# A linear attention, GLU and MLP kernel on one core: weight sums of the GLU stages moved behind a DMA, and one hidden slice's products staged and copied by ScalarE alone

## The chip, the core and the metric

One core of a Trainium2 chip runs the whole program. The metric is device time in microseconds (us). TensorE multiplies matrices, VectorE and ScalarE do elementwise work, GpSimd does elementwise work and issues some of the DMAs (transfers between on-chip memory and DRAM), SyncE (SP) issues the others. Each engine takes its instructions strictly in the order in which the program holds them.

## The reference

```python
x  = linear_attention(q, k, v, omega)     # 4 x 8 heads x 576 tokens x 64 -> 2304 x 512
xn = x / sqrt(mean(x*x, -1) + 1e-6) * rms_g
g  = xn @ w_gate                          # 2304 x 1536
y  = (g * sigmoid(g) * (xn @ w_val)) @ w_out      # 2304 x 512
h  = y @ w2_in                            # 2304 x 2048
out = (h * sigmoid(h)) @ w2_out           # 2304 x 512
```

The weight matrices come as float64, the other arrays as float32.

## The kernel before, in words

**Blocks and slices.** The 2304 tokens are five blocks: 0 to 3 of 512 tokens, and block 4, the short block, of 256. Blocks 0 to 2 are called early (`NE` = 3). The hidden dimension of the GLU is 12 slices f of 128, that of the MLP 16. Each product runs as three TensorE passes (high x high, high x low, low x high), for which each operand is split into a high and a low fp32r half: ScalarE copies the high half (`split_h` L198 for hidden values, `split_hi` L463 for weights, `tok_high` L385 for token sums), and VectorE subtracts it for the low half (L199, L467, L388).

**A weight slice** is loaded by SP as raw words (`raw`), decoded to `m` by five VectorE operations (L146 to L157) and two integer adds on GpSimd (L160), scaled by rms_g on ScalarE (L168, four operations), and split.

**Phases.** Attention and the first two GLU slices run in an order written out by hand until about 180 us. Then the *passage* (`stream`) takes the rest of these slices for blocks 3 and 4 and the third slice, f2, for the blocks in the order 1, 0, 2, 3, 4. For each block there are 12 matmuls each for gate and value (`g1_glu`, `proj`), silu on ScalarE (L222), a multiply on VectorE (L228), the split, and the output product in four quarters of 128 output columns (`g2_glu`, quarters d = 0 to 3, L267). Quarters of blocks 0 and 2 go into a stage tile (`w_2`, `w_3`): even quarters by ScalarE (L278), odd ones by VectorE (L280). After each pair a GpSimd DMA (L281) adds the tile to the block's rows of `out` in DRAM, which serve as an accumulator (`kept`). Those of block 1 are instead added by VectorE to the on-chip tile `ya` (L287), which GpSimd DMAs then write out (L776). The passage also makes four *token sums* of blocks 0 and 1 (L393 adds the halves, L396 and L388 subtract).

**GLU stages.** Slices 3 to 11 are units u = 0 to 8. The four full blocks are done by `quad`, a scheme of seven products for eight that needs the token sums and two *weight sums* (`sum12`, `sum34`: four operations `less` of 128x256 on GpSimd, L362). `WeightQueue.plan` lists the weight jobs of each unit; one job (a tuple) is issued at each tick, between TensorE's pieces. The output products of the unit before (`pend`) are interleaved, and the short block has plain projections (L205) in the middle, with L696 (multiply for the first half) just ahead of the next output product.

**Standard units.** u = 9 is the first MLP unit (`std`); the transition to it is at 555 to 600 us. There `g2_glu` with `last` adds the final slice (L287), and splits the result into `xs` (high by ScalarE, L291, low by `low`, L257: GpSimd for block 1, VectorE otherwise).

`wait` holds the short block's split; `flush` issues it.

Of the kernel before, what the change touches and what calls it, by code (L numbers as in the profile page):

```python
# [20 lines left out]
def kernel(  # L21
# [14 lines left out]
    nc = tc.nc  # L36
# [176 lines left out]
    def proj(w, j, ps):  # L213
        yield 3 * KC * blocks[j] / 2365
        part(w, j, ps, 0, 3 * KC)

    def g1_glu(f, j, hs, mid):
        wq.need((1, "g", f))
        p = ps_tile("ps_g" if blocks[j] == TB * P else "ps_y", [P, blocks[j]])
        yield from proj(wt[1, "g", f], j, p)  # L220
        s = pools["s"][0].tile([P, blocks[j]], F32, tag="s", name="s", bufs=pools["s"][1])
        nc.scalar.activation(out=s, in_=p, func=AF.Silu)  # L222
        if blocks[j] == TB * P:
            yield from mid
        wq.need((1, "v", f))
        p = ps_tile("ps_g" if blocks[j] == TB * P else "ps_y", [P, blocks[j]])
        yield from proj(wt[1, "v", f], j, p)
        nc.vector.tensor_tensor(out=s, in0=s, in1=p, op=ALU.mult)  # L228
        if mid is None:
            wait.append(lambda: hs.update({f: split_h(s, j)}))  # L230
            return
        hs[f] = split_h(s, j)
        if blocks[j] < TB * P:
            yield from mid
# [11 lines left out]
    def kept(j, n):  # L246
        r0 = j * TB * P + 2 * n * P
        return out[r0:r0 + 2 * P, :].rearrange("(p r) d -> p (r d)", r=2)

    def g2_glu(fs, j, hs, first, last, keep=None):  # L250
        wq.need(*[(1, "o", f) for f in fs])
        staged = j < NE and not last and keep is None
        y = ya[j].rearrange("p (c t) -> p c t", c=KC)
        nn = 3 * len(fs)

        def low(d):
            (nc.gpsimd if j == 1 else nc.vector).tensor_tensor(  # L257
                out=xs[j][:, 1, d, :], in0=y[:, d, :],
                in1=xs[j][:, 0, d, :].bitcast(F32), op=ALU.subtract,
            )  # L260

        for d in range(KC):
            ps = ps_tile("ps_y", [P, blocks[j]])
            n = 0
            for f in fs:
                for a, c in PASS:
                    nc.tensor.matmul(  # L267
                        out=ps,
                        lhsT=wt[1, "o", f][:, a, d * P:(d + 1) * P],
                        rhs=hs[f][:, c, :],  # L270
                        start=(n == 0),
                        stop=(n == nn - 1),
                    )
                    n += 1
            if staged:
                if d % 2 == 0:
                    o = stage()
                    nc.scalar.activation(out=o[:, 0, :], in_=ps, func=AF.Copy)  # L278
                else:
                    nc.vector.tensor_copy(out=o[:, 1, :], in_=ps)  # L280
                    nc.gpsimd.dma_start(  # L281
                        out=kept(j, d // 2), in_=o.rearrange("p t d -> p (t d)"), accum_op=ALU.add
                    )
            elif first:
                nc.scalar.activation(out=y[:, d, :], in_=ps, func=AF.Copy)
            else:
                nc.vector.tensor_tensor(out=y[:, d, :], in0=ps, in1=y[:, d, :], op=ALU.add)  # L287
            if keep and d % 2:
                keep(j, d // 2)
            if last:  # L290
                nc.scalar.activation(out=xs[j][:, 0, d, :], in_=y[:, d, :], func=AF.Copy)  # L291
                if d:
                    low(d - 1)
            yield nn * blocks[j] / 2365
        if last:
            low(KC - 1)
# [122 lines left out]
    class WeightQueue:  # L419
# [28 lines left out]
        def plan(self, u):  # L448
# [25 lines left out]
            def lo(key):  # L474
                split_lo(mf(key), st[key].t)
                wt[key] = st[key].t
# [37 lines left out]
            elif kind == 1:  # L514
# [5 lines left out]
                    (1, lambda: hi(a1)),  # L520
                    (0, lambda: lo(a1)),
                    (1, lambda: hi(a0)),
                    (0, lambda: lo(a0), sum12),
                    (0, sum34),
                    (1, lambda: shi(0)),
                    (0, lambda: slo(0), lambda: dec(bs[0], 0), lambda: load(u + 1, 0, 0)),
                    (1, lambda: shi(1)),
# [3 lines left out]
            elif std <= u < std + NSTD:  # L531
# [2 lines left out]
                jobs = [  # L534
                    *head,
                    (0, lambda: dec(a0, 0), lambda: load(u, bs[0], 0)),
                    (0,),
                    (1, lambda: hi(a1)),
                    (0, lambda: lo(a1)),
                    *[(0, lambda: dec(bs[1], 1), lambda: load(u + 1, 1, 1))] * (u > std),  # L540
                    (1, lambda: hi(a0)),
                    (0, lambda: lo(a0)),
                    *[(0, lambda: dec(bs[1], 1), lambda: load(u + 1, 1, 1))] * (u == std),
                    (0, lambda: dec(bs[0], 0), lambda: load(u + 1, 0, 0)),
# [227 lines left out]
    def stream():  # L772
        f0, (f2,) = sweeps[0][1], sweeps[1][1]

        def keep(j, n):
            (nc.gpsimd if j == 1 else nc.sync).dma_start(out=kept(j, n), in_=ya[j][:, 1024 * n:1024 * (n + 1)])  # L776

        for j in (0, 2):
            for n in range(2):
                keep(j, n)  # L780
        pend = ()
        wq.rest = 1.25
        order = [(3, f0), (4, f0), (1, [f2]), (0, [f2]), (2, [f2]), (3, [f2]), (4, [f2])]
# [19 lines left out]
        for n, (j, fs) in enumerate(order):  # L803
# [14 lines left out]
                stages[:] = [wq.slot(("y", k), F32) for k in range(2)]  # L818
            if n == 5:
                sums.extend(later23)  # L820
            out = g2_glu(fs, j, hs, j >= NE and fs is f0, False, keep if j == 1 else None)
            pend = chain_of(pend, flush(), out) if mine else out
        wq.free += [(1, 0), (1, 1)]
        for u, (kind, fs) in enumerate(groups):
            first, last = kind == 2 and fs[0] == 0, u == len(groups) - 1
# [896 lines left out]
```

## Time and profile before

| | |
|---|---|
| runs | 962.07, 962.36, 960.64 us, median 962.07 us |
| profiled execution | 960.27 us; its span 958.5 us |
| TensorE busy | 935.2 us, 98% of the span |
| VectorE | 720.0 us, 75% |
| ScalarE | 524.7 us, 55% |
| GpSimd | 461.8 us, 48% |
| DMA | 128.60 MB, mean 134 GB/s |

The span is that of the profiled execution from its first to its last instruction; the time beside it is the same execution's device time, 1.8 us more. Busy shares are means over phases with different limits. In the timelines below a line gives the start and the length in us, the engine, the source line and the operation as out<-in; several equal instructions in a row are one line (x2), whose length runs from the first one's start to the last one's end; the bracket is the engine's idle time ahead of it and what ended it.

### The profile page before, as it was taken

What the parts mean: (1) busy time and instruction counts of PE and PEld (TensorE: products, weight loads), DVE (VectorE), ACT (ScalarE), POOL (GpSimd) and SP (SyncE); (2) the same over time, 40 slices, a digit from 0 to 9 for tenths busy, and PEclk for the clock granted to TensorE, in tenths of its full rate; (3) what the DMA queues carried; (4) which work ended last, traced back from release to release, by engine and by line L of the source; (5) the groups of instructions that cost most, each with busy time, mean ns of one, the idle gap of its engine ahead of it and who ended that gap; (6) DMA issues with size and microseconds to landing.
All of it is one profiled execution on the core that took longest, in us unless ns stands there. A gap on an engine that the chain in (4) does not pass through costs nothing.

```text
span 958.5 us, 17354 instructions
## 1 busy us (share of the span) xinstructions
PE 935.2 (98%) x6480; PEld 777.8 (81%) x6480; DVE 720.0 (75%) x1335; ACT 524.7 (55%) x1149; POOL 461.8 (48%) x491
## 2 busy tenths in 40 slices
PE   8999999997999999999999998999999999999998
PEld 6888878885788888888888876888888888888887
DVE  6998999777777977877877887977775757575634
ACT  5999877544355355454454445546545444445442
POOL 8888655005335535435434423556544545454411
PEclk9999999998999999999999999999999999999999
DMA  7655443205437658648648650546868787868778
GB/s 186 170 132 148 138 128 100 95 26 152 88 66 162 133 102 175 134 88 185 129 94 184 133 199 1 158 150 131 164 128 169 130 171 129 167 131 160 118 143 172
DMA packets 98500, 128.60 MB, mean 134 GB/s; under 512 B 29424, under 2 KB 75760, under 8 KB 98416
## 3 DMA queue, kind: packets, MB, share of 16 engines
q0 software_dynamic: 17280, 59.78, 35.4%
q1 hardware_dynamic: 80864, 67.65, 25.0%
q8 instruction: 51, 0.84, 0.4%
q14 instruction: 33, 0.27, 0.1%
q10 hardware_dynamic: 272, 0.07, 0.0%
HBM read 54.59 MB, written 68.16 MB: 128 GB/s over the span
## 4 chain that ended last, share of the span: by engine, by line
PE 82%; DVE 8%; ACT 3%; POOL 2%; DMA 2%; issue 1%; SPq 1%; DVEq 0%; POOLq 0%; ACTq 0%
PE g L602 28%; PE y L319 20%; PE y L267 12%; PE g L205 4%; PE b L1190 3%; PE y L205 3%; PE b L205 2%; DVE s L696 2%; PE b L1374 2%; PE kv L1270 2%; PE b L1163 2%; PE b L1590 2%; POOL m L160 1%; ACT h L198 1%; DVE h L199 1%
## 5 line engine op out<-in xcount | busy, mean ns | idle before, releaser
L160 POOL TENSOR_TENSOR m<-m,raw 128x512 int32<-128x512 int32 x136 | 202.8, 1492 | 239.9 <-issue 114.0
L319 PE MATMUL y<-w,h 128*128 128x512 f32 (+1 forms) x870 | 212.2, 388 | 0.6 <-DVE h L199 0.3
L319 PEld LDWEIGHTS y<-w,h 128*128 128x128 f32 x870 | 161.9, 188 | 34.7 <-DVE h L199 0.9
L602 PE MATMUL g<-xs,w 128*128 128x512 f32 x720 | 181.7, 390 | 0.0
L267 PE MATMUL y<-h,w 128*128 128x512 f32 (+1 forms) x648 | 157.1, 377 | 14.7 <-ACT h L198 7.8
L199 DVE TENSOR_TENSOR h<-s,h 128x512 fp32r<-128x512 f32 (+1 forms) x125 | 89.6, 728 | 98.2 <-ACT h L198 98.1
L602 PEld LDWEIGHTS g<-xs,w 128*128 128x128 f32 x720 | 134.2, 188 | 27.3
L267 PEld LDWEIGHTS y<-h,w 128*128 128x128 f32 x648 | 116.0, 192 | 44.3 <-ACT h L198 10.7
L344 POOL DMA_DIRECT2D out_dram<-ya x64 | 58.7, 990 | 116.9 <-DVE ya L338 47.3
L198 ACT ACTIVATE h<-s 128x512 fp32r<-128x512 f32 (+1 forms) x125 | 74.0, 597 | 59.4 <-DVE s L228 27.0
L336 ACT ACTIVATE ya<-y 128x512 f32<-128x512 f32 x82 | 48.2, 593 | 69.0 <-PE y L319 60.2
L205 PE MATMUL g<-xs,w 128*128 128x512 f32 x336 | 80.9, 391 | 0.2 <-DVE xs L257 0.2
L338 DVE COPY ya<-y 128x512 f32<-128x512 f32 x52 | 35.7, 687 | 59.4 <-PE y L319 59.4
L281 POOL DMA_DIRECT2D out_dram<-w x52 | 45.3, 871 | 72.5 <-ACT w L278 68.4
L1239 ACT ACTIVATE e<-b,nb 128x128 f32<-128x128 f32 x272 | 75.8, 423 | 7.5 <-issue 4.1
L205 PEld LDWEIGHTS g<-xs,w 128*128 128x128 f32 x336 | 62.8, 189 | 13.9 <-DVE xs L257 1.0
L614 ACT ACTIVATE g<-g 128x512 f32<-128x512 f32 x60 | 34.9, 581 | 70.7 <-PE g L602 70.1
L467 DVE TENSOR_TENSOR w<-m,w 128x512 fp32r<-128x512 f32 x74 | 69.2, 935 | 3.5 <-ACT w L463 3.5
L629 ACT ACTIVATE s<-s 128x512 f32<-128x512 f32 x42 | 26.6, 632 | 80.0 <-DVE s L634 80.0
L602 PE MATMUL g<-w,w 128*128 128x512 f32 x270 | 69.9, 395 | 0.0
L602 PE MATMUL g<-ya,w 128*128 128x512 f32 x270 | 68.5, 389 | 0.0
L205 PEld LDWEIGHTS y<-xs,w 128*128 128x128 f32 x480 | 60.2, 188 | 2.0
(139 smaller groups left out, 1589.7 us busy)
## 6 DMA issues: line engine op xcount, KB each, us to landing
out_dram<-ya POOLq DMA_DIRECT2D x54, 512.0 KB, 6.8
out_dram<-w POOLq DMA_DIRECT2D x54, 512.0 KB, 7.0
raw<-in_moe_w_out_dram SPq DMA_DIRECT2D x28, 512.0 KB, 4.4
raw<-in_moe_w_in_dram SPq DMA_DIRECT2D x16, 512.0 KB, 4.4
raw<-in_moe_w_gate_dram SPq DMA_DIRECT2D x12, 512.0 KB, 4.1
raw<-in_moe_w_val_dram SPq DMA_DIRECT2D x12, 512.0 KB, 4.6
out_dram<-ya SPq DMA_DIRECT2D x12, 512.0 KB, 5.1
qT<-e SPq DMA_DIRECT2D x72, 64.0 KB, 2.3
```

The source lines that it names most:

```text
L160: tt(out=mi, in0=mi, in1=(low if step == 5 else high).bitcast(I32), op=ALU.add)
L198: nc.scalar.activation(out=ht[:, 0, :], in_=s, func=AF.Copy)
L199: nc.vector.tensor_tensor(out=ht[:, 1, :], in0=s, in1=ht[:, 0, :].bitcast(F32), op=ALU.subtract)
L205: nc.tensor.matmul(out=ps, lhsT=w[:, a, cc * P:(cc + 1) * P], rhs=xs[j][:, c, cc, :], start=(n == 0), stop=(n == 3 * KC - 1),)
L267: nc.tensor.matmul(out=ps, lhsT=wt[1, "o", f][:, a, d * P:(d + 1) * P], rhs=hs[f][:, c, :], start=(n == 0), stop=(n == nn - 1),)
L281: nc.gpsimd.dma_start(out=kept(j, d // 2), in_=o.rearrange("p t d -> p (t d)"), accum_op=ALU.add)
L319: nc.tensor.matmul(out=ps, lhsT=hs[f][:, a, t * P:(t + 1) * P], rhs=wt[2, "p", f][:, c, d0:d1], start=(n == 0), stop=(n == nn - 1),)
L336: nc.scalar.activation(out=o[:, t % 2, :], in_=ps, func=AF.Copy)
L344: nc.gpsimd.dma_start(out=rows, in_=o[p0:p1], accum_op=ALU.add)
L467: eng.tensor_tensor(out=v[:, 1, :], in0=x, in1=v[:, 0, :].bitcast(F32), op=ALU.subtract)
L602: nc.tensor.matmul(out=ps, lhsT=w[:, a, (c0 + c) * P:(c0 + c + 1) * P], rhs=x(b, c), start=(start and n == 0), stop=(n == 3 * KH - 1), ski ...
L1239: nc.scalar.activation(out=st.e[r][:, :, h, :] if blocks4 else st.e[r][:, h, :], in_=src.rearrange("p (a f) -> p a f", a=4) if blocks4 els ...
```

## The change

What the diff does, edit by edit:

1. `proj2` cuts the 12-matmul projections of `g1_glu` into two pieces of 6, so there are more ticks between which other engines' work is issued.
2. Block 1's third slice is staged like those of blocks 0 and 2; its rows are written to `out` early by SP instead of by GpSimd later, and the four VectorE adds (L287) go.
3. `calm`: the third slice's products of blocks 0 to 2 are copied by ScalarE alone.
4. In the plan of a GLU unit (u from 1) `sum12` leaves its job and is issued with `sum34` in the next one.
5. In the plan of unit 9 an empty job goes, and the low half of one weight is issued with the high half of the other.
6. `low` for block 2 goes to GpSimd too.
7. The short block's waiting split is flushed after two quarters of block 3's output product instead of four.

```diff
@@ proj2
+    def proj2(w, j, ps):
+        for n in (0, 6):
+            yield 6 * blocks[j] / 2365
+            part(w, j, ps, n, n + 6)
...
-        yield from proj(wt[1, "g", f], j, p)
+        yield from proj2(wt[1, "g", f], j, p)
...
-        yield from proj(wt[1, "v", f], j, p)
+        yield from proj2(wt[1, "v", f], j, p)
@@ g2_glu
-        staged = j < NE and not last and keep is None
+        staged = j < NE and not last
...
-            (nc.gpsimd if j == 1 else nc.vector).tensor_tensor(
+            (nc.gpsimd if 0 < j < NE else nc.vector).tensor_tensor(
...
-                    nc.scalar.activation(out=o[:, 0, :], in_=ps, func=AF.Copy)
+                if d % 2 == 0 or calm:
+                    nc.scalar.activation(out=o[:, d % 2, :], in_=ps, func=AF.Copy)
                 else:
                     nc.vector.tensor_copy(out=o[:, 1, :], in_=ps)
+                if d % 2:
...
-            if keep and d % 2:
-                keep(j, d // 2)
@@ plan, GLU units
-                    (0, lambda: lo(a0), sum12),
-                    (0, sum34),
+                    (0, lambda: lo(a0)),
+                    (0, sum12, sum34),
@@ plan, standard units
-                    (0,),
+                    *[(0,)] * (u > std),
                     (1, lambda: hi(a1)),
-                    (0, lambda: lo(a1)),
+                    *[(0, lambda: lo(a1))] * (u > std),
...
-                    (1, lambda: hi(a0)),
+                    (1, *[lambda: lo(a1)] * (u == std), lambda: hi(a0)),
@@ stream
-        for j in (0, 2):
+        for j in (0, 2, 1):
             for n in range(2):
-                keep(j, n)
+                nc.sync.dma_start(out=kept(j, n), in_=ya[j][:, 1024 * n:1024 * (n + 1)])
...
-            out = g2_glu(fs, j, hs, j >= NE and fs is f0, False, keep if j == 1 else None)
-            pend = chain_of(pend, flush(), out) if mine else out
+            out = g2_glu(fs, j, hs, j >= NE and fs is f0, False, fs is f0 or j < NE)
+            pend = chain_of(take(pend, 2), flush(), pend, out) if mine else out
```

TensorE's order does not change. The other engines' orders change at three kinds of place. In the rows below, line numbers of the changed kernel are 5 to 8 higher than those of the same statement before.

VectorE in the passage, between the first five decode operations and the multiply and split ahead of block 0's output product. `m` and `raw` are the weight being decoded, `ya_95` is block 1's output tile, `ya_96` and `w_1` are token-sum tiles. Before:

```order
L287 TENSOR_TENSOR ya_95<-y,ya_95 128x512 x2
L396 TENSOR_TENSOR ya_96<-ya_96 128x1024
L287 TENSOR_TENSOR ya_95<-y,ya_95 128x512
L396 TENSOR_TENSOR ya_96<-ya_96,w_1_3921 128x1024
L228 TENSOR_TENSOR s<-s,g 128x512
L199 TENSOR_TENSOR h<-s,h 128x512
L146 TENSOR_SCALAR m_4025<-raw_3974 128x512
```

and in the changed kernel:

```order
L398 TENSOR_TENSOR ya_96<-xs_92 128x1024
L401 TENSOR_TENSOR ya_96<-ya_96 128x1024
L146 TENSOR_SCALAR m_4013<-raw_3962 128x512
L149 TENSOR_SCALAR raw_3962<-raw_3962 128x512
L152 TENSOR_SCALAR m_4013<-m_4013 128x512
L154 TENSOR_SCALAR raw_3962<-raw_3962 128x512
L157 TENSOR_SCALAR m_4013<-m_4013 128x512
L233 TENSOR_TENSOR s<-s,g 128x512
L199 TENSOR_TENSOR h<-s,h 128x512
L401 TENSOR_TENSOR ya_96<-ya_96,w_1_3923 128x1024
```

The four adds to `ya_95` are gone; two token sums (L398 and L401) and the second weight's decode now stand ahead of the multiply (L228, now L233).

ScalarE in the passage, about ten instructions up to the split ahead of block 2's output product. `w_2` and `w_3` are stage tiles, `ya_96` to `ya_4075` token sums. Before:

```order
L198 ACTIVATE h<-s 128x512
L385 ACTIVATE ya_4023<-ya_96 128x1024
L222 ACTIVATE s<-g 128x512
L278 ACTIVATE w_2_3950<-y 128x512
L385 ACTIVATE ya_4055<-ya_96 128x1024
L168 ACTIVATE m_3976<-m_3976,g_sb 128x128 x4
L463 ACTIVATE w_4_4061<-m_3976 128x512
L278 ACTIVATE w_3_3951<-y 128x512
L168 ACTIVATE m_4025<-m_4025,g_sb 128x128 x4
L463 ACTIVATE w_5_4089<-m_4025 128x512
L198 ACTIVATE h<-s 128x512
```

and in the changed kernel:

```order
L198 ACTIVATE h<-s 128x512
L168 ACTIVATE m_3964<-m_3964,g_sb 128x128 x4
L468 ACTIVATE w_4_4039<-m_3964 128x512
L390 ACTIVATE ya_4047<-ya_96 128x1024
L227 ACTIVATE s<-g 128x512
L284 ACTIVATE w_2_3951<-y 128x512 x2
L284 ACTIVATE w_3_3952<-y 128x512
L390 ACTIVATE ya_4075<-ya_96 128x1024
L168 ACTIVATE m_4013<-m_4013,g_sb 128x128 x4
L468 ACTIVATE w_5_4081<-m_4013 128x512
L284 ACTIVATE w_3_3952<-y 128x512
L198 ACTIVATE h<-s 128x512
```

All four copies of block 0's product are now here (L284; two before, L278), the last of them right ahead of the split (L198), and a wait for GpSimd's write of `ya` has no counterpart (the second token sum's copy now comes ahead of the second scale). Block 1's four copies stand in the two rows before this piece.

GpSimd in one GLU stage, with the semaphores that each row waits for; `ws` is the weight sum's tile, `m_4581` and `m_4613` (now `m_4583` and `m_4615`) the two weights. Before:

```order
L281 DMA out_dram<-w_0_4518 128x1024 [waits DMASW5_49,DVE_49,Activation_49]
L281 DMA out_dram<-w_2_3950 128x1024 [waits DMASW6_49,DVE_49,Activation_49]
L362 TENSOR_TENSOR ws<-m_4581 128x256
L362 TENSOR_TENSOR ws<-ws,m_4613 128x256 [waits Pool_49]
L281 DMA out_dram<-w_3_3951 128x1024 [waits DMASW7_49,DVE_49,Activation_49]
L362 TENSOR_TENSOR m_4581<-m_4613,m_4581 128x256
L362 TENSOR_TENSOR m_4581<-m_4613,ws 128x256 [waits Pool_49]
```

and in the changed kernel:

```order
L288 DMA out_dram<-w_0_4520 128x1024 [waits DMASW5_49,DVE_49,Activation_49]
L288 DMA out_dram<-w_2_3951 128x1024 [waits DMASW6_49,DVE_49,Activation_49]
L288 DMA out_dram<-w_3_3952 128x1024 [waits DMASW7_49,DVE_49,Activation_49]
L367 TENSOR_TENSOR ws<-m_4583 128x256
L367 TENSOR_TENSOR ws<-ws,m_4615 128x256 [waits Pool_49]
L367 TENSOR_TENSOR m_4583<-m_4615,m_4583 128x256
L367 TENSOR_TENSOR m_4583<-m_4615,ws 128x256 [waits Pool_49]
```

The last DMA of a stage now stands ahead of the four sums, which follow each other without another instruction between. The same move is in eight stages.

## Rows read from the trace of the kernel before

**Rows 1.** Windows: us; busy PE, PEld, DVE, ACT, POOL; clock; DMA share; GB/s

```profile
200.00:265.00 65.00, 57.90 (x258) 47.15 (x257) 49.80 (x76) 23.61 (x43) 23.84 (x20) 0.92 0.39 98
265.00:555.00 290.00, 286.38 (x1380) 239.39 (x1380) 227.94 (x394) 141.65 (x290) 130.48 (x129) 1.00 0.65 135
555.00:600.00 45.00, 40.84 (x187) 31.98 (x186) 37.72 (x69) 21.50 (x39) 14.64 (x10) 1.00 0.23 83
```

**Rows 2.** What TensorE waited for, whole span; us in total, times, longest

```profile
PE y L267 <- ACT h L198: 7.8, 11, 2.9
```

**Rows 3.** Timeline of TensorE, passage: start, us, engine, line, operation

```profile
221.77 0.50 PE L267 MATMUL y<-h,w 128*128 128x512 f32 x1 [2.10 <-ACT h L198]
...
235.24 0.49 PE L267 MATMUL y<-h,w 128*128 128x512 f32 x1 [2.90 <-ACT h L198]
...
255.56 0.39 PE L267 MATMUL y<-h,w 128*128 128x256 f32 x1 [0.99 <-ACT h L198]
256.60 0.91 PE L267 MATMUL y<-h,w 128*128 128x256 f32 x5 [0.66 <-DVE h L199]
```

**Rows 4.** Windows, the stretch behind the second stall of the passage

```profile
236.80:240.20 3.40, 3.40 (x10) 2.63 (x9) 1.53 (x3) 1.63 (x3) 2.21 (x3) 0.50 0.00 0
```

**Rows 5.** Timeline of all engines, passage, up to the first stall

```profile
212.23 0.69 DVE L287 TENSOR_TENSOR ya<-y,ya 128x512 f32<-128x512 f32 x1 [1.25 <-PE y L267]
212.84 1.22 DVE L388 TENSOR_TENSOR xs<-raw,xs 128x1024 fp32r<-128x1024 f32 x1
...
213.98 0.42 DVE L146 TENSOR_SCALAR m<-raw 128x512 uint32<-128x512 uint32 x1
...
215.66 1.28 DVE L287 TENSOR_TENSOR ya<-y,ya 128x512 f32<-128x512 f32 x2
215.82 3.56 POOL L160 TENSOR_TENSOR m<-m,raw 128x512 int32<-128x512 int32 x2 [40.08 <-DVE m L157]
...
221.09 0.63 ACT L198 ACTIVATE h<-s 128x512 fp32r<-128x512 f32 x1 [8.94 <-DVE s L228]
```

**Rows 6.** Timeline of all engines, passage, up to the second and third stalls

```profile
226.39 1.06 ACT L385 ACTIVATE ya<-ya 128x1024 fp32r<-128x1024 f32 x1 [2.52 <-DMA out_dram<-ya]
...
227.36 1.26 ACT L168 ACTIVATE m<-m,g_sb 128x128 f32<-128x128 f32 x4
...
231.22 0.86 POOL L281 DMA_DIRECT2D out_dram<-w  x1 [2.56 <-ACT m L168]
231.73 2.19 DVE L393 TENSOR_TENSOR w<-xs 128x1024 f32<-128x1024 f32 x1
231.80 1.03 POOL L362 TENSOR_TENSOR ws<-m 128x256 f32<-128x256 f32 x1
232.91 1.60 POOL L362 TENSOR_TENSOR ws<-ws,m 128x256 f32<-128x256 f32 x1
...
255.10 0.41 ACT L198 ACTIVATE h<-s 128x256 fp32r<-128x256 f32 x1
```

**Rows 7.** Timeline of all engines, one of the eight stages

```profile
273.41 0.69 DVE L280 COPY w<-y 128x512 f32<-128x512 f32 x1
...
276.16 2.27 DVE L696 TENSOR_TENSOR s<-s 128x512 f32<-128x512 f32 x1 [0.70 <-ACT s L629]
276.17 1.02 POOL L362 TENSOR_TENSOR m<-m,m 128x256 f32<-128x256 f32 x1
...
279.15 0.49 PE L267 MATMUL y<-h,w 128*128 128x512 f32 x1 [0.23 <-ACT h L198]
```

**Rows 8.** Timeline of all engines, transition to the standard units

```profile
577.88 5.51 POOL L257 TENSOR_TENSOR xs<-ya,xs 128x512 fp32r<-128x512 f32 x4 [6.83 <-ACT xs L291]
...
589.40 0.68 DVE L257 TENSOR_TENSOR xs<-ya,xs 128x512 fp32r<-128x512 f32 x1
```

**Rows 9.** Landing of the accumulating transfers, whole span, then the passage alone

```profile
DMA to landing us min/median/max: 5.2/7.0/9.1
...
DMA to landing us min/median/max: 5.3/5.6/6.7
```

More of the change, by code (lines that the diff above doesn't have):

```diff
@@ L248, in kept, with g2_glu @@
         return out[r0:r0 + 2 * P, :].rearrange("(p r) d -> p (r d)", r=2)
-    def g2_glu(fs, j, hs, first, last, keep=None):
+    def g2_glu(fs, j, hs, first, last, calm=False):
         wq.need(*[(1, "o", f) for f in fs])
-        staged = j < NE and not last and keep is None
+        staged = j < NE and not last
         y = ya[j].rearrange("p (c t) -> p c t", c=KC)
@@ L773, in stream @@
         f0, (f2,) = sweeps[0][1], sweeps[1][1]
-        def keep(j, n):
-            (nc.gpsimd if j == 1 else nc.sync).dma_start(out=kept(j, n), in_=ya[j][:, 1024 * n:1024 * (n + 1)])
-        for j in (0, 2):
+        for j in (0, 2, 1):
             for n in range(2):
-                keep(j, n)
+                nc.sync.dma_start(out=kept(j, n), in_=ya[j][:, 1024 * n:1024 * (n + 1)])
         pend = ()
```

## The prediction

> **What bounds the kernel now.** The page gives TensorE 98% of the span, so I first looked for the stretches where it isn't busy. The windows show three [rows 1]. In the passage (200 to 265 us) it works 57.90 of 65 us, so 7.1 us are idle, and its mean clock is 0.92. In the 290 us of the GLU stages it idles 286.38 against 290, so 3.6 us, at clock 1.00. In the transition to the first standard unit it idles 4.16 of 45 us, also at 1.00. Next I asked what it waits for: the largest entry is ScalarE's high half of a hidden slice, 7.8 us in 11 waits, ahead of an output product [rows 2]. The TensorE timeline of the passage places the long ones: 2.10 at 221.77, 2.90 at 235.24, and 0.99 and 0.66 at 255.56 and 256.60 [rows 3]. The rest of the 7.1 are two waits of 0.23 for the low half behind the first two, like the one in a stage [rows 7].
>
> These stalls cost twice. In the 3.4 us behind the second stall the granted clock is 0.50, the lower level of 1.2 GHz [rows 4], so 1.7 us of work at 2.4 GHz are lost. The mean of 0.92 over 65 us means 5.2 us lost, which is three such stretches, one for each stall place [rows 1]. The stages and the transition show 1.00, so their shorter or more scattered waits don't lower the clock.
>
> The third view is the timeline of all engines around each stall: who is late, and what stood ahead of it in its queue.
>
> **First product of the passage (221.77).** Now: VectorE is free at 210.98 and waits 1.25 for TensorE's first quarter of block 1 before it adds it (L287, 212.23); the other work comes behind this in its queue [rows 5]. Changed: no add to wait for. From 210.98 its queue is one token-sum low half, 1.14 (from 212.84 to 213.98), five decodes, 1.68 (213.98 to 215.66), two token sums, 2.28, and five more decodes, 1.68, which makes 217.8 [rows 5]. GpSimd's two adds behind the first decode take 3.56 [rows 5], and I let VectorE's token sums lose about 2.3 to them, since L393 took 2.19 against 1.22 for an operation of its shape while GpSimd summed [rows 5, 6]. That gives 220.1 for the multiply; with 0.68 for it and 0.63 for ScalarE's split [rows 5] TensorE starts at 221.4. Gain 0.3 here. If VectorE's operations keep their length the product starts when TensorE is ready, at 219.67, without a stall: that is the upper bound, 2.5 us more with the lower clock that then doesn't come.
>
> **Second product (235.24).** Now: ScalarE waits 2.52 for GpSimd's write of `ya` to land before it may overwrite the tile (226.39), and then has the scale (1.26), splits and copies in a row [rows 6]. The change takes away the write, and this wait. It adds six copies for blocks 0 and 1 to ScalarE, which did two of these eight; each is about 0.6 long (estimate from the 0.63 of a split of the same shape [rows 5]). Laid in the changed order: split to 221.4, scale and split of the first weight to 223.2, token copy when VectorE's difference is there (224.4) to 225.5, silu and three copies to 227.45, token copy to 228.4, second scale and split to 230.25. VectorE's low half and multiply take it to 231.55, the split and TensorE's start to 232.3. Against 235.24 that is 2.9 sooner. TensorE itself would be ready at about 232.0 (235.24 less 2.90, less the 0.3 gained before), so 0.3 to 0.5 of a stall is left, as in the stages, where the clock stays up. So the slow stretch behind it goes: 1.7 more.
>
> **Third product (255.56).** Now the short block's split on ScalarE starts at 255.10 [rows 6], behind the silu for the next quad, and the low half comes behind five decodes. In the changed order both stand ahead of these, after the second quarter, some 2 us sooner. The two waits, 1.65 together, go [rows 3], and the slow stretch behind them, 1.7.
>
> Passage: 2.9 + 1.7 + 1.65 + 1.7 = 8.0. What could take from it: two stage tiles now serve blocks 1, 0 and 2, so ScalarE may write one only when its transfer has landed. In the passage a landing takes 5.6, elsewhere up to 9.1 [rows 9]. At 5.6 the tile is free in time, at 9.1 ScalarE waits some 3.4 in the second chain, and the passage brings 4.6. With the upper bound of the first product it brings 10.5. I take 8.0, because the transfers of this stretch are at the short end.
>
> **Stages.** L696 takes 2.27 (276.16), where an operation of its shape takes 0.68 [rows 7, 8]: two sums of GpSimd (1.02 and again 1.01) run beside it [rows 7]. TensorE then waits twice 0.23 for the halves, 0.46 a stage, in eight stages. Changed: the DMA no longer waits behind two sums. The copy that it needs ends at 274.10 [rows 7]; the issue and the hand-over to the next GpSimd instruction take about 0.58 each (231.22 to 231.80 [rows 6]), so the four sums start at 275.25. The first ends at 276.3, shortly after L696 is asked for. In the passage VectorE's L393, asked for during such a first sum (231.73), got its turn at the end of it, and the second sum, asked for at 232.91, took 1.60 [rows 6]. If L696 does the same it ends at about 276.9 rather than 278.43, and ScalarE's half at 277.5. The low half, asked for then, comes at the next change of sums, 278.2, and ends at 278.7, before TensorE wants it at 278.9. So 8 x 0.46 = 3.7 go. If it misses that change it ends at 279.4, and 0.13 a stage remain, 1.0 in all. I take 3.7, since L696 is asked for during the first sum as L393 was; 1.0 and nothing are the lower ends.
>
> Here a rule speaks both ways. The Trainium skill (SBUF — State Buffer, section Who interferes with whom) says that a VectorE instruction with two SBUF inputs contends with a GpSimd one that reads SBUF, and that the one issued first holds the shared pair for its whole instruction. By it, L696 would be next after the first sum and the gain would be the 3.7. The row of L393 agrees (2.19, turn after one sum); L696 at 276.16 as it is now differs, since it lost to two sums in a row.
>
> **Transition.** Block 2's four low halves go from VectorE to GpSimd, about 0.60 of VectorE's queue each, 2.4; on GpSimd four cost 5.51, and it idles 6.83 ahead of block 1's [rows 8]. Against that, the decodes come sooner and stand ahead of adds that TensorE waits for: I find one new wait of some 2.2, and later ones shorter. VectorE's last low half of the full blocks (589.40 [rows 8]) comes about 1.3 sooner, and that is my gain; nothing and 3 are its bounds.
>
> The finer projections (edit 1) cost nothing by themselves: TensorE's 24 matmuls are the same, and their order too.
>
> **Sum.** 8.0 + 3.7 + 1.3 = 13.0. The profiled execution took 960.27 (span 958.5), 1.8 under the median of 962.07. From it I get 947.3, from the median 949.1; I predict 948.2.
>
> **The rivals.**
> *The stages keep their stall.* The four sums run in one block, and the half that VectorE gives up at one place it meets at the next. For it: L696 lost to two sums in a row. Against it: L393 did not. Gain 9.3, 951.5 to 952.
> *Landings are late.* As above, 9.1 instead of 5.6: gain 9.6, 951.5. For it: the median over the whole kernel is 7.0 [rows 9].
> *VectorE wins in the passage.* No first stall and no low clock there: 945.7.
> *The transition gives nothing, or the clock falls there.* Its waits move closer together; 1.3 less and one slow stretch, 1.7, more: 951.
> *Slower.* L696 misses the first change of sums and waits for all four, to about 279.0, so TensorE waits 0.57 more in each stage: 4.6 in eight. The wait is then 1.03, and if the clock falls behind each of them, 8 x 1.7 = 13.6 come on top. With 9.3 from the passage and the transition that is 8.9 slower, about 971. It decides from the point where a stage's wait does to the clock what the 1.65 of the third product did [rows 3]; at 0.46 it does not. For it: L696 lost twice at 276.16.
> *The change doesn't do what it says.* The block of sums holds nobody in the stages because the short block isn't what it waits for; that is the first rival's time.
>
> **How the numbers follow.** Chances: forecast 0.50, stages keep their stall 0.18, late landings 0.12, VectorE wins 0.08, transition 0.07, slower 0.05. The range 943.5 to 956.5 holds the middle four, with the bounds of each term (passage 4.6 to 10.5, stages 0 to 3.7, transition 0 to 3): least 4.6 and half of the rest, most 17. A measurement of this kernel tells about 0.2%, 1.9 us, from no change. All cases but the last are faster by more; some of the low ends together come near to none. So 0.91 faster, 0.04 the same, 0.05 slower.
>
> **What would show it.** In the trace of the changed kernel: between 200 and 265 us a mean clock of about 0.97, one stall of about 2 us before block 0's product, under 0.6 before block 2's, none before the short block's. ScalarE without a wait for a write of `ya`. In the stages, L696 (now L701) at about 0.7 behind a wait, and TensorE without the two 0.23. In the transition the last low half near 588 by before's clock. I'd be wrong if ScalarE's copies waited for landings, if L701 took 2.3 or more, or if TensorE's clock fell in a stretch where it was 1.00.

## The result, and the profile after

The changed kernel takes 950.9 us (median of 4 runs, 947.83 to 951.37) against 961.56 for the kernel before on the same chip. The ratio is 0.9883, 95% interval 0.9859 to 0.9906. The profiled execution is 951.37 us with a span of 949.6, against 960.27 and 958.5.

Windows of the changed kernel over the stretches of [rows 1], and the slow stretch behind the second product of the passage:

```profile
200.00:265.00 65.00, 57.33 (x261) 46.36 (x260) 46.53 (x66) 27.61 (x51) 26.21 (x20) 0.95 0.45 98
265.00:555.00 290.00, 289.98 (x1426) 245.55 (x1425) 227.62 (x408) 143.73 (x293) 143.62 (x133) 1.00 0.68 145
555.00:600.00 45.00, 40.70 (x180) 32.30 (x179) 36.68 (x58) 24.27 (x46) 21.60 (x13) 1.00 0.18 54
236.70:240.10 3.40, 3.40 (x10) 2.64 (x10) 2.81 (x2) 1.35 (x3) 3.40 (x4) 0.57 0.52 101
```

The stages have no idle time left (289.98 of 290). The passage has a little more of it than before, since 57.33 of its 65 us are busy against 57.90, and its clock rose only from 0.92 to 0.95. The stretch behind the second product still runs near the lower of the two levels, 1.2 GHz (0.57, where [rows 4] has 0.50).

What TensorE waits for, whole span: us in total, times, longest:

```profile
PE y L272 <- ACT h L198: 5.2, 2, 3.2
...
PE g L607 <- DVE s L639: 1.5, 2, 1.2
```

ScalarE's high halves go from 7.8 us in 11 waits [rows 2] to 5.2 in 2. Both of these are in the passage. Timeline of TensorE there:

```profile
221.41 0.50 PE L272 MATMUL y<-h,w 128*128 128x512 f32 x1 [1.99 <-ACT h L198]
222.35 4.36 PE L272 MATMUL y<-h,w 128*128 128x512 f32 x11 [0.44 <-DVE h L199]
...
235.35 0.50 PE L272 MATMUL y<-h,w 128*128 128x512 f32 x1 [3.20 <-ACT h L198]
236.25 4.35 PE L272 MATMUL y<-h,w 128*128 128x512 f32 x11 [0.40 <-DVE h L199]
...
254.65 1.24 PE L272 MATMUL y<-h,w 128*128 128x256 f32 x6
...
259.76 1.66 PE L607 MATMUL g<-w,w 128*128 128x512 f32 x6 [0.39 <-DVE s L639]
...
263.93 1.65 PE L607 MATMUL g<-xs,w 128*128 128x512 f32 x6 [1.15 <-DVE s L639]
```

The first two stalls are where they were in [rows 3], at 1.99 and 3.20. The third is gone: the short block's product at 254.65 starts without a wait. Two others are new, 0.39 and 1.15, both in the first stage and for L639, VectorE's add of two of the `quad` scheme's products (`plus`); in VectorE's queue it stands behind the decode of a weight. The same passage on the other engines:

```profile
211.97 2.64 ACT L284 ACTIVATE w<-y 128x512 f32<-128x512 f32 x4
...
213.96 4.46 POOL L160 TENSOR_TENSOR m<-m,raw 128x512 int32<-128x512 int32 x2 [38.49 <-DVE m L157]
...
215.05 2.21 DVE L401 TENSOR_TENSOR ya<-ya 128x1024 f32<-128x1024 f32 x1
...
217.19 1.53 DVE L146 TENSOR_SCALAR m<-raw 128x512 uint32<-128x512 uint32 x1
...
218.38 2.04 POOL L288 DMA_DIRECT2D out_dram<-w  x2
...
226.03 1.09 ACT L284 ACTIVATE w<-y 128x512 f32<-128x512 f32 x2 [1.41 <-PE y L272]
...
229.88 0.60 ACT L284 ACTIVATE w<-y 128x512 f32<-128x512 f32 x1 [2.76 <-DMA out_dram<-w]
...
234.67 0.63 ACT L198 ACTIVATE h<-s 128x512 fp32r<-128x512 f32 x1 [0.94 <-DVE s L233]
```

ScalarE has copied block 1's four quarters by 214.6. GpSimd is at the first weight's two adds from 213.96 to 218.42, and only then issues both accumulating transfers, one right behind the other from 218.38 on. The landing of these two:

```profile
DMA to landing us min/median/max: 7.6/9.0/10.3
```

The slower is the second. ScalarE waits 2.76 for it, to 229.88, before it can copy block 0's third quarter into the same stage tile, and its split for block 2 comes at 234.67.

One stage on all engines, with the same place in the next stage:

```profile
273.65 0.86 POOL L288 DMA_DIRECT2D out_dram<-w  x1 [0.60 <-issue]
...
274.22 1.06 POOL L367 TENSOR_TENSOR ws<-m 128x256 f32<-128x256 f32 x1
...
274.94 2.99 PE L205 MATMUL y<-xs,w 128*128 128x256 f32 x24
275.17 0.69 DVE L701 TENSOR_TENSOR s<-s 128x512 f32<-128x512 f32 x1 [0.70 <-ACT s L634]
275.36 1.10 POOL L367 TENSOR_TENSOR ws<-ws,m 128x256 f32<-128x256 f32 x1
...
277.77 2.92 PE L272 MATMUL y<-h,w 128*128 128x512 f32 x12
...
309.21 2.99 PE L205 MATMUL y<-xs,w 128*128 128x256 f32 x24
```

Before, TensorE's short-block projections of these two stages started here:

```profile
275.93 2.99 PE L205 MATMUL y<-xs,w 128*128 128x256 f32 x24
...
311.19 2.99 PE L205 MATMUL y<-xs,w 128*128 128x256 f32 x24
```

A stage lasts 34.27 from projection to projection, and lasted 35.26: 0.99 less, where the two waits make only 0.46. The transition, TensorE's two longest waits:

```profile
558.12 0.73 PE L205 MATMUL g<-xs,w 128*128 128x512 f32 x2 [2.19 <-DVE xs L262]
...
574.45 1.22 PE L272 MATMUL y<-h,w 128*128 128x256 f32 x6 [1.62 <-DVE ya L294]
```

To place the gain I compared the starts of the same TensorE instruction in both traces at four points and at the last matmul (before: 200.26, 275.93, 557.98 and 596.16, all first matmuls of projections). Us by which each kernel's stretch is longer (+) or shorter than that of the kernel before:

| kernel | passage | eight stages | transition | after it |
|---|---|---|---|---|
| after | -0.7 | -7.6 | -0.8 | +0.1 |
| sums_only | -0.1 | -7.8 | 0.0 | -0.2 |
| no_sums | -1.7 | +0.7 | -0.8 | +0.4 |
| no_early_flush | +3.2 | -7.6 | -1.1 | -0.1 |
| block1_not_staged | -4.7 | -7.6 | -1.0 | 0.0 |
| no_fine_proj | -2.6 | -7.6 | -1.0 | 0.0 |
| block1_in_own_tile | +1.2 | -7.6 | -0.8 | 0.0 |
| own_tile_no_fine_proj | +2.7 | -7.6 | -1.0 | 0.0 |
| no_std_plan | -0.7 | -7.9 | -1.4 | -0.1 |
| dma_before_adds | -6.6 | -7.6 | -0.7 | +1.0 |
| dma_before_adds_no_fine_proj | -8.4 | -7.6 | -1.1 | 0.0 |
| that_and_old_std_plan | -8.5 | -7.9 | -1.7 | +1.1 |
| low2_on_vector | -1.5 | -7.6 | +0.8 | +0.3 |

The stretch up to 200 us differs by -2.7 to +2.5 between these executions. All of it arises before 150 us, ahead of every edit, so it is left out of the table; it is also why a difference of 1 or 2 us between two times says little. The table places 9.0 us for the changed kernel, where the medians differ by 10.7.

### The profile page after: what moved, and what is told of

Read it like the earlier page. It is cut to its first block, busy times and chain, and to the rows that moved or that the text cites. A ratio compares the mean times of both kernels' runs of the same rounds, so it can differ in the third digit from the quotient of the medians.

```text
span 949.6 us, 17368 instructions
## 1 busy us (share of the span) xinstructions
PE 929.1 (98%) x6480; PEld 776.0 (82%) x6480; DVE 709.4 (75%) x1323; ACT 530.7 (56%) x1157; POOL 477.5 (50%) x495
## 4 chain that ended last, share of the span: by engine, by line
PE 86%; DVE 7%; ACT 3%; POOL 2%; issue 1%; DMA 1%; SPq 0%; DVEq 0%; ACTq 0%; POOLq 0%
PE g L607 28%; PE y L324 20%; PE y L272 12%; PE y L205 5%; PE g L205 4%; PE b L1192 4%; PE b L205 4%; PE b L1376 2%; PE kv L1272 2%; PE b L1165 2%; PE b L1592 2%; POOL m L160 1%; DVE ya L294 1%; DMA out_dram<-w 1%; PE b L1352 1%
## 5 line engine op out<-in xcount | busy, mean ns | idle before, releaser
L199 DVE TENSOR_TENSOR h<-s,h 128x512 fp32r<-128x512 f32 (+1 forms) x125 | 95.0, 771 | 97.8 <-ACT h L198 97.7
L272 PE MATMUL y<-h,w 128*128 128x512 f32 (+1 forms) x648 | 152.9, 373 | 8.0 <-ACT h L198 5.2
L198 ACT ACTIVATE h<-s 128x512 fp32r<-128x512 f32 (+1 forms) x125 | 74.0, 597 | 42.7 <-DVE s L233 20.3
L288 POOL DMA_DIRECT2D out_dram<-w x54 | 47.9, 893 | 82.9 <-ACT w L284 78.1
```

The source lines that it names most:

```text
L198: nc.scalar.activation(out=ht[:, 0, :], in_=s, func=AF.Copy)
L199: nc.vector.tensor_tensor(out=ht[:, 1, :], in0=s, in1=ht[:, 0, :].bitcast(F32), op=ALU.subtract)
L272: nc.tensor.matmul(out=ps, lhsT=wt[1, "o", f][:, a, d * P:(d + 1) * P], rhs=hs[f][:, c, :], start=(n == 0), stop=(n == nn - 1),)
L288: nc.gpsimd.dma_start(out=kept(j, d // 2), in_=o.rearrange("p t d -> p (t d)"), accum_op=ALU.add)
```

## The experiments

The kernel before ran beside each group; a ratio is to it.

**The sums alone.** In the kernel before, only edit 4:

```diff
-                    (0, lambda: lo(a0), sum12),
-                    (0, sum34),
+                    (0, lambda: lo(a0)),
+                    (0, sum12, sum34),
```

> The kernel before with the weight sums behind the last DMA of a stage, and nothing else. Theory (the trace of after: every one of the eight stages gets 0.97 shorter, twice 0.23 of wait and twice about 0.26 for the first matmul behind a wait): 7.7 us under the kernel before, about 954. Rival (the stage's wait of 0.46 is all that this edit brings, and the rest comes from the other edits): 3.7 under it, about 958.

953.29 us against 961.32, ratio 0.992 (0.9903 to 0.9937), 7.7 us by the ratio. Its stages in the windows:

```profile
265.00:555.00 290.00, 290.00 (x1426) 245.85 (x1426) 225.87 (x405) 144.79 (x294) 140.91 (x131) 1.00 0.68 143
```

The theory holds: this edit alone makes the eight stages 7.8 shorter, and changes nothing elsewhere.

**The change without the sums.** The same lines put back in the changed kernel.

> The changed kernel with the weight sums put back ahead of the last DMA. Theory: the eight stages get their two waits back, 7.7 us over the changed kernel, about 958.5. Rival (only 0.46 a stage): 3.7 over it, about 954.5.

959.35 us, ratio 0.9987 (0.9973 to 1.0002): the changed kernel without this edit can't be told from the kernel before. Its eight stages are 8.3 longer than the changed kernel's. TensorE's waits for the high half are back, 10 of them (and as many for the low half):

```profile
PE y L272 <- ACT h L198: 6.7, 10, 2.5
```

**The short block's flush as before.**

```diff
-            pend = chain_of(take(pend, 2), flush(), pend, out) if mine else out
+            pend = chain_of(pend, flush(), out) if mine else out
```

> The changed kernel with the short block's split flushed after four quarters, as before. Theory (the stall before the short block's product and the slow clock behind it, 3.3 us and a refill, went, but two new waits of 0.39 and 1.15 at VectorE's sums in the first GLU stage took back 2 of it): 1 to 2 us over the changed kernel, with the stall at the short block's product and without the new ones. Rival (the two new waits come from other edits and stay): 3.3 or more over it.

955.76 us, ratio 0.9946 (0.993 to 0.9963). The passage is 3.9 longer than in the changed kernel. TensorE at the short block's product:

```profile
258.58 0.38 PE L272 MATMUL y<-h,w 128*128 128x256 f32 x1 [0.99 <-ACT h L198]
261.29 1.44 PE L272 MATMUL y<-h,w 128*128 128x256 f32 x5 [2.33 <-DVE h L199]
```

There the low half is waited for 2.33, where it was 0.66 [rows 3]. It stands behind the same five decodes in both traces, but here VectorE begins them 1.0 after ScalarE's split begins (259.15 against 258.12), and in the kernel before it had begun them 0.65 ahead of it. The two waits for L639 are gone, as the theory said, but the stall is twice what I had taken, so the edit is worth 3.9 and not 1 to 2. In size the rival was nearer.

**Block 1 not staged.** Its product is added by VectorE (L294) and written by GpSimd, as before; the rest of the change stays:

```diff
-        staged = j < NE and not last
+        staged = j < NE and not last and keep is None
...
+            if keep and d % 2:
+                keep(j, d // 2)
...
+        def keep(j, n):
+            (nc.gpsimd if j == 1 else nc.sync).dma_start(out=kept(j, n), in_=ya[j][:, 1024 * n:1024 * (n + 1)])
...
-        for j in (0, 2, 1):
+        for j in (0, 2):
```

> The changed kernel with block 1's third product added by VectorE and written by GpSimd, as before; ScalarE alone still copies blocks 0 and 2. Theory (in the changed kernel ScalarE waits 2.76 for the landing, 10.3 us long, of block 1's second accumulating transfer before it can copy block 0's third quarter, so the product of block 2 starts no sooner than before): without that transfer the copy has no such wait, the wait for the write of the token tile may come back instead (2.5 before), and the time is between 3 under and 1 over the changed kernel. Rival (the second product is late for VectorE's and ScalarE's queues, not for the landing): same time or slower by 1 to 3, with TensorE's wait at block 2's product still about 3 and no wait of ScalarE for a landing.

946.93 us, ratio 0.9857 (0.9836 to 0.9878), against 950.9 for the changed kernel on the first chip. Its passage is 3.9 shorter than the changed kernel's:

```profile
227.00 0.60 ACT L284 ACTIVATE w<-y 128x512 f32<-128x512 f32 x1 [0.36 <-PE y L272]
...
233.76 2.88 PE L272 MATMUL y<-h,w 128*128 128x512 f32 x12
```

ScalarE copies the third quarter when TensorE has it (0.36), and block 2's product at 233.76 doesn't wait at all. Part of this is that TensorE itself comes later, since the first stall grew to 3.05; but the product also starts 1.6 sooner than the changed kernel's, with the same start of the passage (199.99 and 200.00). This speaks for the landing as what made block 2's product late; the run also takes four copies from ScalarE, and dma_before_adds below does not.

**Projections in one piece.** Edit 1 taken back (`proj` for `proj2` in `g1_glu`):

> The changed kernel with the 12-matmul projections in one piece again. In its order the second weight's five decodes and their two GpSimd adds come behind the multiply and split of block 0, not ahead of them. Theory (the finer pieces bring these decodes forward into the chain ahead of block 0's product, so they are what keeps the first stall): the wait of 2.0 and 0.4 before block 0's product and the slow clock behind it go, about 3 to 4 us, but the wait for the landing stays, with a stall before block 2's product; together 1 to 4 us under the changed kernel. Rival (the finer pieces cost nothing, as the prediction said): same time, within 1 us.

948.94 us, ratio 0.9892 (0.9871 to 0.9912); the passage is 1.9 shorter than the changed kernel's. The first stall is gone, and the second is more than twice as long:

```profile
218.05 2.33 POOL L288 DMA_DIRECT2D out_dram<-w  x2
...
226.94 0.60 ACT L284 ACTIVATE w<-y 128x512 f32<-128x512 f32 x1 [7.15 <-DMA out_dram<-w]
...
234.68 4.64 PE L272 MATMUL y<-h,w 128*128 128x512 f32 x12 [7.42 <-ACT h L198]
```

ScalarE now comes to block 0's first copy sooner and waits 7.15 there, for the first of the same two transfers. The theory holds: the finer pieces make the first stall, and the landing caps what its removal gives.

**Block 1 in its own tile.**

```diff
-                    o = stage()
+                    o = ya[1][:, 512 * d:512 * (d + 2)].rearrange("p (t d) -> p t d", t=2) if calm and j == 1 else stage()
...
-                tag = f"ya{(1, 0, 2)[n - 2]}"
+                tag = f"ya{(0, 1, 2)[n - 2]}"
```

> The changed kernel, but block 1's third product is staged in that block's own on-chip tile, whose rows SP has written out by then, instead of in the two stage tiles; the token sums take their tiles in another order, so that the first of them doesn't wait for this tile. The same transfers are issued. Theory (ScalarE's wait is for the stage tile, not for anything else): ScalarE copies block 0's third quarter without the wait of 2.76, block 2's product comes 2 to 3 us sooner, no slow clock behind it: 3 to 5 us under the changed kernel, at or under the kernel whose block 1 isn't staged. Rival (four transfers of 512 KB in a row hold up the later chain anyway, by loads that land late): within 1.5 us of the changed kernel.

952.92 us, ratio 0.9935 (0.9915 to 0.9956): slower than the changed kernel, so here neither side was right.

```profile
217.63 2.04 POOL L288 DMA_DIRECT2D out_dram<-ya  x2
...
227.88 1.06 ACT L390 ACTIVATE ya<-ya 128x1024 fp32r<-128x1024 f32 x1 [5.44 <-DMA out_dram<-ya]
...
235.75 5.96 PE L272 MATMUL y<-h,w 128*128 128x512 f32 x12 [4.50 <-ACT h L198]
```

The wait has moved. ScalarE no longer waits for the stage tile, but the second token-sum copy (227.88) goes into the tile from which block 1 is being sent, and waits 5.44 for the same transfers. So the landing is the cause, and another tile helps only where nobody wants it next.

**Both together.**

> Both of the above: block 1 in its own tile, and the projections in one piece. Theory: no stall before block 0's, block 2's and the short block's products, clock 1.00 in most of the passage; 6 to 8 us under the changed kernel, about 943 to 945. Rival (the time that the one gives is what the other gives too, since the later waits at the first GLU stage's token sums take it back): as the better of the two alone.

953.83 us, ratio 0.9939 (0.9915 to 0.9962). ScalarE's wait for this landing is 11.25 here, and TensorE's at block 2's product 11.37. This expectation was wrong for the same reason.

**The plan of the first standard unit as before.**

```diff
-                    *[(0,)] * (u > std),
+                    (0,),
                     (1, lambda: hi(a1)),
-                    *[(0, lambda: lo(a1))] * (u > std),
+                    (0, lambda: lo(a1)),
...
-                    (1, *[lambda: lo(a1)] * (u == std), lambda: hi(a0)),
+                    (1, lambda: hi(a0)),
```

> The changed kernel with the plan of the first standard unit as before; block 2's low halves stay on GpSimd. Theory (the earlier decodes make the new wait of 2.2 at the start of the transition, which takes most of what the four low halves bring): 1 to 2.5 us under the changed kernel. Rival (the decodes have to come sooner, or the adds of the last slice are late by them as before): 1 to 2 us over it.

949.48 us, ratio 0.9897 (0.9876 to 0.9918), which can't be told from the changed kernel's 0.9883. In the trace the wait of 2.19 is gone and others stand in its place:

```profile
558.21 1.66 PE L272 MATMUL y<-h,w 128*128 128x512 f32 x6 [1.13 <-DVE ya L294]
...
571.43 0.62 PE L272 MATMUL y<-h,w 128*128 128x256 f32 x3 [1.08 <-DVE ya L294]
```

The transition is 0.7 shorter than with the new plan, less than was expected, and neither the theory nor the rival is shown.

**The transfers ahead of the adds.** In the changed kernel the first weight's decode is issued two jobs later, so that GpSimd has block 1's transfers ahead of this weight's adds:

```diff
                 jobs = [
-                    (0, lambda: dec(a0, 0), lambda: load(u, bs[0], 0)),
                     (0,),
                     (0,),
+                    (0, lambda: dec(a0, 0), lambda: load(u, bs[0], 0)),
                     (0, lambda: dec(a1, 1), lambda: load(u + 1, 1, 1)),
```

> The changed kernel with the first weight's decode of the passage two jobs later, so that GpSimd issues the two accumulating transfers of block 1 ahead of this weight's two adds; everything else is the same. Theory (the transfers are late because GpSimd issues them behind adds of 4.46 us, at 218.4 and 219.2, and both land late; ScalarE waits for the second one): they are issued about 4 us sooner, ScalarE's wait of 2.76 before block 0's third quarter goes, block 2's product comes 2 to 3 us sooner without the slow clock behind it; the stall before block 0's product stays. 3 to 5 us under the changed kernel in the traces, ratio to the kernel before about 0.984. Rival (a pair of such transfers takes 10 us however early, and the decode that now comes later makes the chain ahead of block 0's product longer): same time or slower, ratio 0.988 or over.

947.09 us, ratio 0.9862 (0.984 to 0.9883). Block 1's transfers, the adds and the copies of block 0's next quarters:

```profile
214.33 2.21 POOL L288 DMA_DIRECT2D out_dram<-w  x2 [38.10 <-ACT w L284]
...
216.25 3.27 POOL L160 TENSOR_TENSOR m<-m,raw 128x512 int32<-128x512 int32 x2
...
225.24 1.56 ACT L284 ACTIVATE w<-y 128x512 f32<-128x512 f32 x3
```

and the landing of these two transfers:

```profile
DMA to landing us min/median/max: 5.7/7.0/8.4
```

They are issued from 214.33, land after 5.7 and 8.4, and ScalarE copies three quarters in a row at 225.24 without a wait. TensorE has no stall at block 2's product, and the passage is 5.9 shorter than the changed kernel's. This moved no work to another engine and took none away. VectorE's order changes with it, since the decode stands behind one token sum more, but block 0's product still waits 1.95. So it is the order on GpSimd's queue that cost this.

**The same, with projections in one piece.**

> The same, with the projections in one piece, so that the second weight's decode and adds come behind block 0's multiply and split. Theory (the first stall is for these decodes and for GpSimd's adds beside them, the second for the late landing): neither stall, clock near 1.00 in the whole passage; 6 to 9 us under the changed kernel, ratio about 0.980. Rival (a chain later on, the token copies and scales on ScalarE, then ends last and makes a stall of its own at block 2's product): ratio 0.985 to 0.989.

943.09 us, ratio 0.9824 (0.9805 to 0.9843), the lowest ratio of all. The passage in the windows, TensorE's products for the blocks 0 and 2 in its timeline, and the landing of block 1's transfers:

```profile
200.00:265.00 65.00, 61.74 (x293) 50.31 (x292) 50.41 (x76) 35.57 (x69) 24.90 (x21) 1.00 0.46 106
```

```profile
219.06 0.39 PE L272 MATMUL y<-h,w 128*128 128x512 f32 x1
219.61 2.79 PE L272 MATMUL y<-h,w 128*128 128x512 f32 x11 [0.15 <-DVE h L199]
...
229.06 0.50 PE L272 MATMUL y<-h,w 128*128 128x512 f32 x1 [1.22 <-ACT h L198]
229.78 1.43 PE L272 MATMUL y<-h,w 128*128 128x512 f32 x5 [0.22 <-DVE h L199]
```

```profile
DMA to landing us min/median/max: 5.5/6.1/6.7
```

The clock is 1.00, 61.74 of 65 us are busy, and the waits at these two products are 0.15, 1.22 and 0.22. The passage is 8.4 shorter than before. The prediction had 8.0 for it, but by other terms: the first stall, which it kept, is gone here, and the two waits for L639, which it did not have, stand as in the changed kernel (0.39 and 1.14).

**And with the old plan of the first standard unit.**

> The one before, and the plan of the first standard unit as it was. Theory (the plan's earlier decodes make the wait of 2.2 at the start of the transition): about 1 us under the one before. Rival (the plan makes no difference in sum): within 0.5 us of it.

943.01 us, ratio 0.9828 (0.9808 to 0.9848): the same. The rival holds. In its trace the transition gains 0.6 and the rest loses 1.1, with a wait of 0.66 for the high half at 632.47. That is not shown to be the old plan's doing: dma_before_adds, with the new plan, has such a wait too (0.52 at 634.89) and loses 1.0 there.

**Block 2's low halves on VectorE.** Edit 6 taken back:

```diff
-            (nc.gpsimd if 0 < j < NE else nc.vector).tensor_tensor(
+            (nc.gpsimd if j == 1 else nc.vector).tensor_tensor(
```

> The changed kernel with block 2's low halves back on VectorE, its plan of the first standard unit kept. Theory (the four low halves stand ahead of adds that TensorE waits for): 1 to 3 us over the changed kernel, ratio to the kernel before about 0.991, with longer waits for the adds between 558 and 580. Rival (VectorE isn't what ends last there, and GpSimd's low halves, 1.4 each, only hold the shared port): same time as the changed kernel, ratio 0.988.

952.19 us, ratio 0.9917 (0.9899 to 0.9935). Its transition is 1.6 longer than the changed kernel's:

```profile
555.00:600.00 45.00, 40.81 (x173) 32.33 (x172) 37.57 (x61) 22.98 (x43) 14.80 (x9) 0.96 0.16 43
```

But the waits there are the changed kernel's (2.09 and 1.62), and the clock of this window is 0.96, which over 45 us is the loss of about one slow stretch, 1.8. The changed kernel's trace has 1.00 behind a wait as long (2.19). But no_sums, which has edit 6, shows a slow stretch there as well: 0.57 from 566 to 570 us, behind a wait of 2.08. So the slow stretch doesn't come from taking edit 6 back, and this run doesn't show the longer waits for the adds that the theory wanted. That edit 6 brings anything is not shown.

## Why the prediction was right, and where not

The time lies in the range, 2.7 over the forecast, and its parts are off in both directions: -0.7, -7.6 and -0.8 were measured for -8.0, -3.7 and -1.3. (The range's upper end is not the sum that it is said to be: 4.6 and half of the rest, 2.5, give about 954 and not 956.5. The measured time lies inside either.)

**Passage: the step on the landing failed.** "At 5.6 the tile is free in time" took the landing of before's single transfers for that of a pair, and gave their issue no time. Both transfers stand behind the first weight's adds on GpSimd; I counted these adds in VectorE's chain (3.56, measured 4.46) and not in GpSimd's own queue. The transfers were issued at 218.38 and 219.17 and took 7.6 and 10.3. By an estimate from these times it took both to make ScalarE wait: it wanted the tile at 227.1, and 5.6 from 219.17 would have been in time (224.8), as would 10.3 from dma_before_adds' issue at 215.68 (226.0). The late-landing rival had the landing but not the issue, with 9.1 and 4.6 left of the gain. It left too much, because with the stall at 3.20 the slow stretch stays too. dma_before_adds shows the cause: with the same transfers issued about 4 us sooner the stall and the slow stretch go.

The first product came at 221.41, as forecast (221.4), but the 2.3 that the sum let token sums lose to GpSimd's adds was lost in other places: 1.0 by one of them (L401, 2.21 for 1.22) and 1.1 by a decode (L146, 1.53 for 0.42). The third product's wait went as forecast, but the step had nothing after it: the two waits for L639 took back about 2 (1.54 together, and some 0.26 behind each, by the price below). TensorE had been too late to meet them before.

**Edit 1 "costs nothing": wrong.** TensorE's order is the same, but the ticks between the pieces set where the others' work is issued. no_fine_proj shows that they bring the second weight's decode ahead of block 0's multiply, and with it the first stall: without them it is gone, and the passage is 1.9 shorter.

**Stages: the mechanism was right, the term too small.** L701, asked for during the first sum, starts at 275.17 as that one ends, and takes 0.69 for 2.27; the second sum gives way (1.10). The forecast was 2.27 cut to the turn behind one sum, and this is what the rows show, so the rivals in which the sums hold VectorE longer are out. The row that the forecast leaned on, L393, carries less than it took from it: it starts at 231.73, 0.07 ahead of its sum [rows 6] and not during it. L701's row agrees with the Trainium skill (SBUF — State Buffer, section Who interferes with whom): a VectorE instruction with two SBUF inputs and a GpSimd one that reads SBUF exclude each other, and the one issued first has the pair for its whole instruction. L696's 2.27 before, behind two sums, does not. What the term missed is what a wait costs behind itself. The first matmul after a wait takes 0.49 [rows 7], where 12 in a row take 2.92, the last one's own length included, so that one starts every 0.23. Hence each of the two waits costs 0.23 and about 0.26 more, and a stage 0.98 by these rows; the table's 7.6 over eight stages is 0.95 each. sums_only gave 7.7 us by itself, no_sums took it away.

**Transition: direction right, size open.** 0.8 for 1.3, with the new wait of 2.19 that the working had at 2.2. What each edit there brings is less than these runs can tell, as the last experiment shows. Edit 3, the copies done by ScalarE alone, wasn't tried by itself.

So the sum came near by luck: a term forecast at half its size covered for one forecast ten times too large. What the passage lacked is in reach: with GpSimd's transfers ahead of the adds and the projections in one piece, the kernel is at 943.09, ratio 0.9824, against 0.9883 for the change.

## What to carry to other kernels

When a result is handed from an engine to a DMA that another engine issues, follow it into the issuing engine's queue: what stands ahead of it there delays the landing, and the next writer of the tile meets it. Price a wait of TensorE by the whole distance between the same instructions with and without it, not by the idle time alone: here a wait of 0.23 cost 0.49. Finer pieces of the same work are an edit to every other engine's order, so read that order before calling them free.

## What the runs showed of the hardware

Two accumulating transfers of 512 KB issued one right behind the other, after GpSimd's adds, landed after 7.6 and 10.3 us, and two after 5.5 and 6.7 in the best kernel, where they were issued sooner and 1.35 us apart instead of 0.79; single ones took 5.3 to 6.7 in the passage before [rows 9]. The distance alone isn't the cause: in dma_before_adds they were 1.35 apart as well, and took 5.7 and 8.4. In the kernel before, GpSimd issued two plain writes of 512 KB 0.78 apart at this place, and they took 5.8 and 6.2. What else was being moved differs between these traces, so the cause stays open.

The clock did not follow the length of a wait in a simple way. It stayed at 1.00 behind 1.22 and 0.22 in the best kernel's passage, and fell behind 0.99 and 0.66 in the kernel before [rows 3], to 0.50 from 257.3 to 260.7 us. Behind the wait of about 2.1 in the transition it stayed at 1.00 in the changed kernel's trace (2.19), and fell in low2_on_vector's (2.09; 0.96 over the window) and in no_sums' (2.08; 0.57 over 4 us).
